# Three convolution steps among the gates of a fused convolution and feed-forward kernel: behind units 1, 5 and 9 in place of 1, 3 and 5

## The chip, the cores and the metric

The kernel runs on one core of one Trainium2 chip. The metric is the device time of one execution in microseconds. A profiled execution gives every instruction of the five engines: TensorE (PE, with its weight loads as PEld), VectorE (DVE), ScalarE (ACT), GpSimd (POOL) and SyncE (SP), which issues transfers here.

## The reference

Two blocks in a row, in float32:

```
# x: (8, 4096, 192), weight: (8, 7)
w = softmax(weight, axis=-1)
out[b, s, d] = sum_k w[head(d), k] * x_padded[b, s + k, d]     # causal, 7 taps, 8 heads of 24 channels

# tokens: 8 * 4096 = 32768, w_in: (192, 2048), w_out: (2048, 192)
h = out.reshape(32768, 192) @ w_in
g = h * clip(h + 3, 0, 6) / 6                                    # hardswish
return g @ w_out
```

## The kernel before, in words

The 32768 tokens are taken in 32 blocks of 1024. A block has two groups of 512 tokens, which lie in the lower and the upper 64 partitions. The first block (number 0) has a path of its own with the preparation of the weights. Blocks 1 to 31 go through the same two stages, which are the 31 iterations of the loop at the end of the kernel.

**The first layer** (`first_layer`) computes h and the gate. It has 16 units, 8 with the tokens as they lie (`y_own`) and 8 with the two groups swapped (`y_other`). Each unit makes 128 features for both groups. A float32 product is made of three parts in a 32-bit format for TensorE: `HIGH`, `LOW` and `MIX`. `begin(n)` takes a pair of PSUM banks, issues the 12 matmuls of HIGH and LOW (L510) and scales the sum on ScalarE (L521). `end(n)` adds the 6 matmuls of MIX, then clamps on ScalarE (`relu`, L302) and multiplies on VectorE (`gate`, L306). The gate reads the pair of banks; when it has ended, the pair is free. There are four pairs. TensorE's order is begin(0), begin(1), and then end(n), begin(n + 2) for each n, but begin(15) comes ahead of end(13). So begin(n + 4) waits for gate n.

**The sums of gates.** Both layers' products are organised in a Strassen-like way with fewer products and more sums. Behind units 1, 3, 5 and 7 GpSimd makes `small_sums` (L573, four instructions each) of the two units just gated. Behind units 9, 11 and 13 it makes a sum `g_sums` (L414), and behind 9 and 11 it also issues a transfer that adds one part of g onto another (L552). VectorE makes that sum behind unit 15.

**The second layer** (`second_layer`) multiplies by `w_out` (L609), sums the parts, transposes and stores. Its order is written out by hand with due times. VectorE has most of its sums there (L573, L414, L458), and also splits the next block's y into its three parts (L877, L479).

**The convolution** of block i + 1 runs on VectorE during block i. Its seven steps go through the whole of `y` (128 partitions x 1536). The first is a scaled copy on ScalarE (L859), and the other six are multiply-adds on VectorE, in place, one tap each (L861):

```
            for k in range(1, KC):
                jobs.append(lambda k=k: nc.vector.scalar_tensor_tensor(
                    out=y[:], in0=x[:, :, k : k + N], scalar=c_sb[:, k : k + 1], in1=y[:],
                    op0=ALU.mult, op1=ALU.add,
                ))
```

Steps 1 and 2 are done at the end of the second layer. Step 3 comes ahead of the first gate, with two last output sums of the block before (`left`). Steps 4, 5 and 6 are `conv[4:]`, handed to `first_layer` as `jobs`, a table from unit to what follows its gate. The order of every engine's queue is the order in which the kernel issues (a manual schedule): each engine takes its instructions one after the other.

Of the kernel before, what the change touches and what calls it, by code (L numbers as in the profile page):

```python
# [25 lines left out]
def kernel(  # L26
# [50 lines left out]
    def load_x(i, dma=nc.sync):  # L77
        x = xs.tile([P, K3, PAD + N], F32, name="x")
        head, lower, upper = x_source(i)
        if head:  # L80
            nc.vector.memset(x[0:D2, :, 0:PAD], 0.0)
        dma.dma_start(out=x[0:D2, :, head:], in_=lower)
        dma.dma_start(out=x[D2:P, :, :], in_=upper)
        return x
# [655 lines left out]
    with tc.manual_schedule():  # L740
# [82 lines left out]
        n = 3  # L823
# [33 lines left out]
        def conv_jobs(i):  # L857
            x = x_tiles.pop(i)
            jobs = [lambda: nc.scalar.mul(y[:], x[:, :, 0:N], c_sb[:, 0:1])]  # L859
# [5 lines that stand above are left out]
            return jobs  # L865
# [35 lines left out]
        conv = conv_jobs(2)  # L901
        conv[0]()
        left = conv[1:3]
        for i in range(1, NB):
            jobs = {2 * n + 1: [job] for n, job in enumerate(conv[4:])}
            jobs[-1] = left + conv[3:4]
            first_layer(i, jobs)
            conv = []

            def begin_conv():  # L910
                x_tiles[i + 2] = load_x(i + 2)
                conv.extend(conv_jobs(i + 2))

            between = []
            if i + 1 < NB:
                between = [(13, split_high), (15, split_rest), (18, swap_parts)]
            if i + 2 < NB:
                between += [(20, begin_conv), (60, lambda: conv[0]()), (72, lambda: conv[1]()), (73, lambda: conv[2]())]
            left = second_layer(i, between)
# [33 lines left out]
```

## Time and profile before

| | us |
|---|---|
| device time, median of 3 runs (2244.72 to 2244.84) | 2244.84 |
| span of the profiled execution | 2244.1 |
| one iteration, from the chain of waits (237.99 to 306.94 is one) | 68.95 |
| of it the second layer on TensorE (216 pieces in the chain) | 35.47 |
| of it the first layer on TensorE, the rest | 33.48 |
| convolution step on VectorE (L861), least, median, longest | 1.774, 1.820, 2.249 |
| gate on VectorE (L306), median | 1.220 |
| clamp on ScalarE (L302), mean in the groups of the page | 1.088 |

How to read it: TensorE's row says where the time is, because the whole span is TensorE's stream, one iteration after the other. The other engines' rows only matter where they make TensorE wait. A line of a timeline has the start, the length, the engine, the line of the kernel, the operation, what it writes and reads, how many instructions are merged into it, and in brackets the idle time ahead of it with the one that ended it. In a table of waits the columns are the total, the number of times and, where there is one, the longest.

### The profile page before, as it was taken

What the parts mean: (1) busy time and instruction counts of PE and PEld (TensorE: products, weight loads), DVE (VectorE), ACT (ScalarE), POOL (GpSimd) and SP (SyncE); (2) the same over time, 40 slices, a digit from 0 to 9 for tenths busy, and PEclk for the clock granted to TensorE, in tenths of its full rate; (3) what the DMA queues carried; (4) which work ended last, traced back from release to release, by engine and by line L of the source; (5) the groups of instructions that cost most, each with busy time, mean ns of one, the idle gap of its engine ahead of it and who ended that gap; (6) DMA issues with size and microseconds to landing.
All of it is one profiled execution on the core that took longest, in us unless ns stands there. A gap on an engine that the chain in (4) does not pass through costs nothing.

```text
span 2244.1 us, 50173 instructions
## 1 busy us (share of the span) xinstructions
PE 2233.8 (100%) x21432; PEld 1525.2 (68%) x21432; DVE 1890.1 (84%) x1636; ACT 1388.8 (62%) x1676; POOL 825.0 (37%) x689
## 2 busy tenths in 40 slices
PE   9999999999999999999999999999999999999998
PEld 5467776676766667766767667676666776676765
DVE  8888888888898888888888888889888888888876
ACT  7457665576655676555766556665567655576653
POOL 2444432344422444323443224442244432344322
PEclk9999999999999999999999999999999999999999
DMA  6344224443234342344423443323434234443332
GB/s 155 71 84 83 48 58 91 86 81 64 54 79 91 78 80 46 68 90 83 84 51 60 85 89 78 70 52 74 90 79 85 46 62 90 84 83 55 58 69 34
DMA packets 254063, 166.57 MB, mean 74 GB/s; under 512 B 208528, under 2 KB 213648, under 8 KB 253840
## 3 DMA queue, kind: packets, MB, share of 16 engines
q1 hardware_dynamic: 235416, 129.53, 28.3%
q0 software_dynamic: 17184, 33.57, 8.6%
q8 instruction: 168, 2.75, 0.5%
q14 instruction: 55, 0.45, 0.1%
q10 hardware_dynamic: 1240, 0.27, 0.1%
HBM read 31.72 MB, written 25.17 MB: 25 GB/s over the span
## 4 chain that ended last, share of the span: by engine, by line
PE 98%; DVE 1%; ACT 0%; issue 0%; DVEq 0%; ACTq 0%
PE psum L609 49%; PE psum L510 44%; PE psum L296 2%; PE psum L341 2%; DVE g L306 1%; DVE y L861 1%; PE psum L755 0%; PE psum L763 0%; ACT g L302 0%; DVE results L458 0%; ACT psum L521 0%; DVE results L464 0%; ACT results L709 0%; DVE zeros L111 0%; DVEq L464 0%
## 5 line engine op out<-in xcount | busy, mean ns | idle before, releaser
L609 PE MATMUL psum<-g,w_out 128*32 128x512 f32 (+1 forms) x6696 | 967.3, 553 | 0.0
L306 DVE SCALAR_TENSOR_TENSOR g<-g,psum 128x1024 f32<-128x1024 f32 (+1 forms) x528 | 611.9, 1183 | 224.4 <-ACT g L302 220.0
L573 POOL TENSOR_TENSOR s<-g 128x256 f32<-128x256 f32 x248 | 318.8, 1285 | 1213.6 <-DVE g L306 1213.6
L302 ACT ACTIVATE g<-psum,half 128x1024 f32<-128x1024 f32 (+1 forms) x528 | 564.7, 1088 | 0.8
L521 ACT ACTIVATE psum<-psum 128x1024 f32<-128x1024 f32 x496 | 500.2, 1009 | 74.9 <-PE psum L510 72.0
L609 PEld LDWEIGHTS psum<-g,w_out 128*32 128x32 f32 x6696 | 370.0, 110 | 247.0 <-issue 127.9
L510 PE MATMUL psum<-y_other,w_in 64*128 64x512 f32 x4464 | 530.6, 390 | 1.3
L510 PE MATMUL psum<-y,w_in 64*128 64x512 f32 x4464 | 521.9, 388 | 0.0
L510 PEld LDWEIGHTS psum<-y,w_in 64*128 64x128 f32 x4464 | 413.7, 184 | 116.3 <-issue 25.1
L510 PEld LDWEIGHTS psum<-y_other,w_in 64*128 64x128 f32 x4464 | 411.3, 184 | 110.3 <-DVE g L306 22.1
L609 PE MATMUL psum<-s,w_out 128*32 128x512 f32 (+1 forms) x3224 | 465.4, 576 | 0.0
L861 DVE SCALAR_TENSOR_TENSOR y<-x,c_sb,y 128x1536 f32<-128x1536 f32 x186 | 360.5, 1938 | 1.3
L609 PE MATMUL psum<-g,w_s 128*32 128x256 f32 x1240 | 282.8, 379 | 0.0
L414 POOL TENSOR_TENSOR s<-g 128x1024 f32<-128x1024 f32 x93 | 224.6, 2415 | 67.2 <-DVE g L306 67.2
L609 PEld LDWEIGHTS psum<-s,w_out 128*32 128x32 f32 x3224 | 152.5, 110 | 81.7 <-issue 50.0
L609 PEld LDWEIGHTS psum<-g,w_s 128*32 128x32 f32 x1240 | 136.4, 110 | 67.8
L414 DVE TENSOR_TENSOR s<-g 128x2048 f32<-128x2048 f32 (+1 forms) x93 | 179.4, 1957 | 1.1
L609 PE MATMUL psum<-s,w_s 128*32 128x256 f32 x744 | 170.7, 379 | 0.0
L573 DVE TENSOR_TENSOR g<-g 128x1024 f32<-128x1024 f32 x124 | 151.7, 1224 | 5.2
L414 DVE TENSOR_TENSOR g<-g 128x2048 f32<-128x2048 f32 x62 | 139.1, 2284 | 0.0
L606 ACT COPY psum<-psum 32x512 f32<-32x512 f32 x93 | 51.3, 551 | 132.7 <-PE psum L609 132.7
L458 DVE TENSOR_TENSOR results<-psum,results 32x256 f32<-32x256 f32 (+1 forms) x125 | 68.0, 544 | 48.4 <-issue 47.0
(82 smaller groups left out, 1266.6 us busy)
## 6 DMA issues: line engine op xcount, KB each, us to landing
y_other<-y SPq DMA_DIRECT2D x186, 384.0 KB, 5.1
g<-g POOLq DMA_DIRECT2D x62, 512.0 KB, 5.0
out_dram<-results SPq DMA_DIRECT2D x378, 64.0 KB, 2.0
x<-in_x_dram SPq DMA_DIRECT2D x53, 388.5 KB, 7.7
stage<-in_moe_w_in_dram SPq DMA_DIRECT2D x16, 192.0 KB, 4.5
stage<-in_moe_w_out_dram SPq DMA_DIRECT2D x8, 384.0 KB, 5.2
x<-in_x_dram SPq DMA_DIRECT2D x7, 384.0 KB, 8.4
x<-in_x_dram POOLq DMA_DIRECT2D x2, 388.5 KB, 5.8
```

The lines of the kernel that those rows point to most:

```text
L296: nc.tensor.matmul(out=psum[:, b], lhsT=w[r], rhs=src, start=start, stop=stop, skip_group_check=onto,)
L302: nc.scalar.activation(r6, h, ACT.Relu, bias=half[:], scale=1.0 / 6.0)
L306: nc.vector.scalar_tensor_tensor(out=g_, in0=g_, scalar=1.0, in1=h, op0=ALU.min, op1=ALU.mult)
L341: lambda p=p: nc.tensor.matmul(out=bank[j * QS : (j + 1) * QS, tokens], lhsT=w_out[:, p, w, cols], rhs=x[:, p, tokens], start=(first and p ...
L414: engine.tensor_tensor(out=o[:, r], in0=a[:, r], in1=b[:, r], op=op)
L458: nc.vector.tensor_tensor(out=out, in0=x, in1=y, op=op)
L510: nc.tensor.matmul(out=psum[:, 2 * slots[n] + k], lhsT=r32(w_in_parts[part][r, c, s]), rhs=r32(y_other[0][r, part, s] if group else y_own[ ...
L521: nc.scalar.mul(both(n), both(n), 4097.0)
L573: engine.tensor_tensor(out=o, in0=p, in1=q, op=op)
L606: streams[3].append((t - 0.5, lambda: fn(*args, **kw)))
L609: nc.tensor.matmul(out=out, lhsT=w, rhs=x, start=start, stop=True, tile_position=(0, j * QS), skip_group_check=True,)
L861: jobs.append(lambda k=k: nc.vector.scalar_tensor_tensor(out=y[:], in0=x[:, :, k : k + N], scalar=c_sb[:, k : k + 1], in1=y[:], op0=ALU.mu ...
```

## The change

In each iteration the steps 4, 5 and 6 of the convolution follow other gates. Before, they came behind the gates of units 1, 3 and 5. Now they come behind those of units 1, 5 and 9. What is computed, and the order of the six steps among themselves, stays. The purpose is to spread VectorE's work in the first layer: two gates stand between two steps before, and four now.

```diff
         for i in range(1, NB):
-            jobs = {2 * n + 1: [job] for n, job in enumerate(conv[4:])}
+            jobs = {4 * n + 1: [job] for n, job in enumerate(conv[4:])}
             jobs[-1] = left + conv[3:4]
             first_layer(i, jobs)
```

The orders of TensorE, ScalarE, GpSimd and SyncE are the same in both kernels. Only VectorE's differs. Its queue in the first layer, one iteration, by lines of the kernel:

```
before:  L306 x2, L861, L306 x2, L861, L306 x2, L861, L306 x10
after:   L306 x2, L861, L306 x4, L861, L306 x4, L861, L306 x6
```

## The prediction

> **What bounds the kernel now.** I read four views in this order: the page's busy shares, the chain of waits, the table of waits, and the timeline of one of the 31 repeated iterations, engine by engine. The page first:
>
> ```profile
> PE 2233.8 (100%) x21432; PEld 1525.2 (68%) x21432; DVE 1890.1 (84%) x1636; ACT 1388.8 (62%) x1676; POOL 825.0 (37%) x689
> PEclk9999999999999999999999999999999999999999
> PE 98%; DVE 1%; ACT 0%; issue 0%; DVEq 0%; ACTq 0%
> ```
>
> TensorE carries 98% of the chain at full clock. Only holes in its stream can be won, and a busy share of 100% with modelled ends hides them. The table of waits, kept to weight loads, lists them:
>
> ```profile
> PEld psum L510 <- issue: 25.1, 30, 0.8
> PEld psum L510 <- DVE g L306: 22.7, 61, 0.5
> PEld psum L510 <- ACT psum L521: 5.2, 31, 0.2
> ```
>
> 61 times a first-layer weight load waits for a gate (L306): the gate frees the PSUM pair that the unit four later writes. That wait is what the change can reach. One iteration's weight loads show its size:
>
> ```profile
> 1148.98 0.64 PEld L510 LDWEIGHTS psum<-y,w_in 64*128 64x128 f32 x6
> 1149.90 1.23 PEld L510 LDWEIGHTS psum<-y_other,w_in 64*128 64x128 f32 x12 [0.28 <-DVE g L306]
> 1151.17 0.65 PEld L510 LDWEIGHTS psum<-y,w_in 64*128 64x128 f32 x6
> 1151.86 2.00 PEld L510 LDWEIGHTS psum<-y_other,w_in 64*128 64x128 f32 x18
> 1154.33 0.75 PEld L510 LDWEIGHTS psum<-y_other,w_in 64*128 64x128 f32 x8 [0.47 <-DVE g L306]
> ```
>
> Loads come in pairs, one for each half of the rows. Nine pairs take 2.04 us (this is the spacing of units everywhere between the stalls), so 0.227 us a pair. The third pair of the first line starts at 1148.98 + 2 x 0.227 = 1149.43; the next is due at 1149.66 and comes at 1149.90: 0.24 us lost, in front of unit 8. The ninth pair from 1151.86 starts at 1153.68; the next is due at 1153.90 and comes at 1154.33: 0.42 us lost, in front of unit 10. The idle times in brackets are some 0.04 us above the loss each, which is the ordinary hole between two pairs. So the 61 waits cost about 22.7 - 61 x 0.043 = 20.1 us.
>
> Why VectorE is late, from its own timeline and GpSimd's:
>
> ```profile
> 1142.47 1.81 DVE L861 SCALAR_TENSOR_TENSOR y<-x,c_sb,y 128x1536 f32<-128x1536 f32 x1
> 1144.20 2.37 DVE L306 SCALAR_TENSOR_TENSOR g<-g,psum 128x1024 f32<-128x1024 f32 x2
> 1146.49 2.23 DVE L861 SCALAR_TENSOR_TENSOR y<-x,c_sb,y 128x1536 f32<-128x1536 f32 x1
> 1148.64 2.34 DVE L306 SCALAR_TENSOR_TENSOR g<-g,psum 128x1024 f32<-128x1024 f32 x2
> 1150.90 2.24 DVE L861 SCALAR_TENSOR_TENSOR y<-x,c_sb,y 128x1536 f32<-128x1536 f32 x1
> 1153.06 2.34 DVE L306 SCALAR_TENSOR_TENSOR g<-g,psum 128x1024 f32<-128x1024 f32 x2
> 1158.08 1.22 DVE L306 SCALAR_TENSOR_TENSOR g<-g,psum 128x1024 f32<-128x1024 f32 x1 [1.15 <-ACT g L302]
> 1160.15 1.22 DVE L306 SCALAR_TENSOR_TENSOR g<-g,psum 128x1024 f32<-128x1024 f32 x1 [0.85 <-ACT g L302]
> ```
>
> ```profile
> 1142.63 2.25 POOL L573 TENSOR_TENSOR s<-g 128x256 f32<-128x256 f32 x1 [40.23 <-DVE g L306]
> 1144.96 0.75 POOL L573 TENSOR_TENSOR s<-s,g 128x256 f32<-128x256 f32 x1
> 1147.05 2.27 POOL L573 TENSOR_TENSOR s<-g 128x256 f32<-128x256 f32 x1
> 1158.12 0.75 POOL L573 TENSOR_TENSOR s<-g,s 128x256 f32<-128x256 f32 x1
> 1159.38 2.41 POOL L414 TENSOR_TENSOR s<-g 128x1024 f32<-128x1024 f32 x1 [0.51 <-DVE g L306]
> ```
>
> Two gates (2.34 us) and a step (2.24 us) need about 4.4 us from step to step (1146.49 to 1150.90), while TensorE makes two units in 4.08. Three steps in a row build a backlog. In the second half of the stage VectorE waits 0.8 to 1.15 us before each gate: the room is there.
>
> **What the Trainium skill says.** "SBUF — State Buffer", section "Who interferes with whom": a VectorE instruction with two SBUF inputs contends with a GpSimd instruction that reads SBUF, and whichever issues first keeps the shared port for its whole length. The trace agrees. The step at 1142.47, ahead of GpSimd's, takes 1.81 us and stretches that one from 0.75 to 2.25; the steps at 1146.49 and 1150.90 meet a GpSimd instruction under way and take 2.23. Gates, with one input in PSUM, stay at 1.22. "TensorE: Matmul & The Clock Gate", section "Back-to-back issue gap", gives 518 cycles for an isolated 512-column matmul at 2.4 GHz, 0.216 us; the trace's pair takes 0.227, and I use the trace.
>
> **The change part by part.** Nothing is added or removed, and only VectorE's queue is reordered: the step behind unit 3 goes behind 5, and the one behind 5 goes behind 9. No other engine's order changes.
>
> First the allowance. The ScalarE clamp (L302) of unit 4 ends at 1147.36, and clamps follow each other by 2.04 (starts 1148.29, 1150.33). Call the end R(n): R(4) = 1147.36, R(5) = 1149.40, R(6) = 1151.44, R(9) = 1157.56, R(10) = 1159.60 without stalls. Unit 8 is due at 1149.66, some 0.05 after gate 4 must end: a gate has until R + 2.25. Alone it ends at R + 0.04 + 1.22 = R + 1.26. So gate n has 0.99 us to spare, plus what gate n-1 leaves.
>
> Step behind 1: as now. Gate 2 starts at 1144.20, ends at 1145.41 = R(2) + 2.13, within 2.25, and no stall stands there today.
>
> Step behind 3, taken away: gate 4 starts at R(4) + 0.04 and ends at 1148.62 instead of 1149.85. The 0.24 us before unit 8 goes.
>
> Step behind 5: gate 5 ends at 1150.66 and the step starts 0.08 before that, at 1150.58. GpSimd's small sums of units 2 and 3 start at about 1147.05, no longer stretched, and 4 x 0.70 us later, at 1149.9, they are done. So the step finds the port free and takes 1.81, to 1152.39. Gate 6 starts 0.08 earlier and ends at 1153.53 = R(6) + 2.09. Unit 10 is due at 1153.74, allowing for no earlier stall, and gate 6 needs to end by 1153.69: 0.16 to spare. The 0.42 us goes.
>
> Step behind 9: gate 9 ends at 1158.82, the step starts at 1158.74. The small sums of units 6 and 7 start behind those of 4 and 5 at 1155.2 and end at 1158.0, 0.7 before it. The GpSimd sum (L414) that waits for gate 9 starts 0.08 after that gate's end, so 0.16 after the step: the order of 1142.47 and 1142.63 again. The step runs 1.81 us, gate 10 ends at R(10) + 2.09, and unit 14 isn't held.
>
> What is queued behind this step: gates 10 to 15 on VectorE. Gate 11 is due at R(11) + 1.26 and follows gate 10 without loss, so unit 15, which is taken ahead of the end of unit 13, has 0.3 us more than its gate needs. On GpSimd the sum of 2.41 us is held until 1160.55 and ends near 1162.9 instead of 1161.80. Then an accumulating transfer is issued (0.30 + 1.21), the next sum runs to about 1166.9, and its transfer is issued by 1168.4 where 1167.39 stands now; with 5.0 us to landing it is there by about 1172.5. VectorE reads these sums at 1178.07 now, 1177.4 then: 5 us to spare. The last GpSimd sum then starts at about 1168.6 and ends near 1171.0; VectorE's own sum, ready at 1170.5, may wait 0.5 us for the port. VectorE waits 0.1 and 0.2 us in the second layer at 1179 and 1180.8, which takes up most of that, and its product sums (two of 2.3 us from 1184.13) still end about a microsecond ahead of their use. I cost all this at nothing.
>
> Sum: in iterations 2 to 30 both stalls go, 29 x 0.66 = 19.2 us. Iteration 1 has three (0.39, 0.17 and 0.34 us by the same reading); the first two come from five VectorE instructions and a step in front of gate 0 and stay, the third goes. Iteration 31 has no steps and no stall today. 19.2 + 0.34 = 19.5 us; 2244.84 - 19.5 = 2225.3.
>
> **The rivals.** (a) Half a gain: the allowance of 0.16 us isn't enough, or a GpSimd instruction is under way when a moved step starts, as for 2.23-us steps today. Each of the two moved steps then costs up to 0.24 us: 30 x 0.48 = 14.4 of the 19.5 come back, 2239.7. For it: the allowance is thin. Against: gate 2 makes do with 0.12 in every iteration.
> (b) Nothing: the gates come earlier but TensorE meets another wait one step on, for instance ScalarE, whose two instructions fill 2.04 us of every 2.04. Against: the only such wait shown is 5.2 us in all, with the last unit. It would give 2244.8.
> (c) Slower: GpSimd's sum wins the port before the step behind 9. The step waits until 1158.90 + 2.41 = 1161.31 and ends at 1163.1, gate 10 at 1164.2 against an allowance of 1161.85: 2.35 us x 30 = 70 less the 19.5, 2295. Against: VectorE starts its next instruction before the last one's recorded end, GpSimd 0.08 after it.
>
> **How the numbers follow.** Full gain 0.80, (a) 0.08, (b) 0.04, (c) or a late sum in the second layer 0.08. The forecast is 2225.3. The low end is the removal of every gate stall, 2224.7, with a margin for the reading, 2223.0. The high end allows each of the three steps 0.1 us over the allowance, 30 x 0.3 = 9 us: 2234.5. (b) and (c) and the full size of (a) lie outside, 0.20. Faster: 0.80 + 0.08 = 0.88; same 0.04; slower 0.08.
>
> **What would show it.** Right: waits of L510 for gates fall from 61 to about 2, and from 22.7 to under 1 us; all three steps last about 1.8 us; the first layer falls from 33.44 to about 32.8 us and the second stays at 35.5; the first GpSimd sum (L414) stretches to about 4 us. Wrong: a step of 2.2 us or more behind 5 or 9, a new wait of L510 or L609 for VectorE or GpSimd, or a longer second layer.

## The result and the profile after

The changed kernel takes 2230.24 us (median of 6, 2230.07 to 2230.50) against 2244.81 us (median of 6, 2244.52 to 2245.09): 14.6 us less, ratio 0.9935, 95% interval 0.9922 to 0.9948. The forecast was 2225.3 us in a range of 2223.0 to 2234.5.

The page of the changed kernel, the lines that answer to those of before:

```profile
PE 2219.4 (100%) x21432; PEld 1528.0 (69%) x21432; DVE 1872.5 (84%) x1636; ACT 1390.0 (62%) x1676; POOL 827.7 (37%) x689
PEclk9999999999999999999999999999999999999999
PE 100%; DVE 0%; issue 0%; ACT 0%; DVEq 0%
```

VectorE has left the chain of waits. The table of waits of the weight loads (total, times, longest):

```profile
PEld psum L510 <- issue: 26.0, 31, 0.8
PEld psum L510 <- ACT psum L521: 10.3, 62, 0.2
PEld psum L510 <- DVE g L306: 1.1, 3, 0.5
```

Of 61 waits for a gate 3 are left, all in iteration 1. The other waits were there before. ScalarE's row had 31 times and has 62, because a second hole of each iteration, ahead of the MIX part of unit 0, was 0.146 us and is 0.166, and only now the table lists it.

Where the time came from, in the chain of waits. First before, then after, two neighbouring stages of each (start, length, what):

```profile
1134.14 20.15 PE psum L510 x174
1154.28 0.04 issue
1154.33 13.27 PE psum L510 x114
1167.60 35.47 PE psum L609 x216
```

```profile
1058.24 32.92 PE psum L510 x288
1091.17 35.47 PE psum L609 x216
```

The second layer is 35.47 us in both. The first layer is 33.46 us before and 32.92 after: 0.54 us in each of iterations 2 to 30, 15.7 in all, which is the difference of the two profiled spans (2244.1 and 2228.4). The profiled execution of before was 1.3 us above the median of its kernel (2246.07 against 2244.81) and that of the changed kernel 0.3 above (2230.50 against 2230.24), so the medians differ by a little less, 14.6.

VectorE in the first layer of a later iteration of the changed kernel, and GpSimd beside it, from the timeline:

```profile
1134.95 1.81 DVE L861 SCALAR_TENSOR_TENSOR y<-x,c_sb,y 128x1536 f32<-128x1536 f32 x1
1143.06 1.81 DVE L861 SCALAR_TENSOR_TENSOR y<-x,c_sb,y 128x1536 f32<-128x1536 f32 x1
1144.79 2.43 DVE L306 SCALAR_TENSOR_TENSOR g<-g,psum 128x1024 f32<-128x1024 f32 x2
1151.22 1.81 DVE L861 SCALAR_TENSOR_TENSOR y<-x,c_sb,y 128x1536 f32<-128x1536 f32 x1
1152.95 2.44 DVE L306 SCALAR_TENSOR_TENSOR g<-g,psum 128x1024 f32<-128x1024 f32 x2
```

```profile
1141.76 0.74 POOL L573 TENSOR_TENSOR s<-g,s 128x256 f32<-128x256 f32 x1
1143.22 2.25 POOL L573 TENSOR_TENSOR s<-g 128x256 f32<-128x256 f32 x1 [0.73 <-DVE g L306]
1149.86 0.74 POOL L573 TENSOR_TENSOR s<-g,s 128x256 f32<-128x256 f32 x1
1151.39 3.92 POOL L414 TENSOR_TENSOR s<-g 128x1024 f32<-128x1024 f32 x1 [0.79 <-DVE g L306]
```

All three steps last 1.81 us. GpSimd has been idle for 0.73 and 0.79 us when its next sum is released, so the two moved steps find it at rest and start 0.16 us ahead of it. Then GpSimd waits: one sum is 2.25 us long instead of 0.74, and the sum for units 8 and 9 is 3.92 instead of 2.41. The transfer behind that sum is issued later for it, but no load or matmul waits for GpSimd here.

### The profile page after: what moved, and what is told of

Same layout as the page of the kernel before. It is cut to its first block, busy times and chain, and to the rows that moved or that the text cites. A ratio compares the mean times of both kernels' runs of the same rounds, so it can differ in the third digit from the quotient of the medians.

```text
span 2228.4 us, 50173 instructions
## 1 busy us (share of the span) xinstructions
PE 2219.4 (100%) x21432; PEld 1528.0 (69%) x21432; DVE 1872.5 (84%) x1636; ACT 1390.0 (62%) x1676; POOL 827.7 (37%) x689
## 4 chain that ended last, share of the span: by engine, by line
PE 100%; DVE 0%; issue 0%; ACT 0%; DVEq 0%
PE psum L609 49%; PE psum L510 46%; PE psum L296 2%; PE psum L341 2%; PE psum L755 0%; PE psum L763 0%; DVE results L458 0%; DVE results L464 0%; ACT results L709 0%; DVE zeros L111 0%; DVEq L464 0%; DVE x L96 0%; DVE half L233 0%; DVE bias_e L150 0%; DVE bias_e L149 0%
## 5 line engine op out<-in xcount | busy, mean ns | idle before, releaser
L306 DVE SCALAR_TENSOR_TENSOR g<-g,psum 128x1024 f32<-128x1024 f32 (+1 forms) x528 | 618.1, 1186 | 228.2 <-ACT g L302 223.9
L573 POOL TENSOR_TENSOR s<-g 128x256 f32<-128x256 f32 x248 | 271.6, 1095 | 1232.3 <-DVE g L306 1232.3
L510 PE MATMUL psum<-y,w_in 64*128 64x512 f32 x4464 | 521.7, 388 | 0.0
L510 PE MATMUL psum<-y_other,w_in 64*128 64x512 f32 x4464 | 517.0, 386 | 0.0
L510 PEld LDWEIGHTS psum<-y,w_in 64*128 64x128 f32 x4464 | 413.3, 184 | 116.1 <-issue 26.0
L510 PEld LDWEIGHTS psum<-y_other,w_in 64*128 64x128 f32 x4464 | 415.7, 184 | 91.0 <-ACT psum L521 5.1
L861 DVE SCALAR_TENSOR_TENSOR y<-x,c_sb,y 128x1536 f32<-128x1536 f32 x186 | 336.1, 1807 | 1.3
L414 POOL TENSOR_TENSOR s<-g 128x1024 f32<-128x1024 f32 x93 | 282.7, 3040 | 30.2 <-DVE g L306 30.2
```

The lines of the kernel that those rows point to most:

```text
L306: nc.vector.scalar_tensor_tensor(out=g_, in0=g_, scalar=1.0, in1=h, op0=ALU.min, op1=ALU.mult)
L414: engine.tensor_tensor(out=o[:, r], in0=a[:, r], in1=b[:, r], op=op)
L510: nc.tensor.matmul(out=psum[:, 2 * slots[n] + k], lhsT=r32(w_in_parts[part][r, c, s]), rhs=r32(y_other[0][r, part, s] if group else y_own[ ...
L573: engine.tensor_tensor(out=o, in0=p, in1=q, op=op)
L861: jobs.append(lambda k=k: nc.vector.scalar_tensor_tensor(out=y[:], in0=x[:, :, k : k + N], scalar=c_sb[:, k : k + 1], in1=y[:], op0=ALU.mu ...
```

## The experiments

**What makes a gate late: the number of gates between two steps, or GpSimd?** Both fit the result. The spacing theory says that three steps with two gates between them are too much by themselves. The port theory says that they are too much only because a step that meets a GpSimd instruction which reads SBUF is held up. With the order of before, two gates and a step needed 4.4 us against 4.08, but two of the steps took 2.23 us instead of 1.81. The cleanest test keeps the order of before and takes away what GpSimd reads.

```diff
-                small_sums(s1[-1], A11, (1, 2, 3, 4), nc.gpsimd, every[n - 1 : n + 1])
+                nc.gpsimd.memset(s1[-1][:, n - 1 : n + 1], 0.0)
```

> The order of before (1, 3, 5), with the GpSimd small sums of the first layer left out: a GpSimd memset of their destination stands in their place, which reads nothing. Port theory: all three steps take about 1.8 us, two gates and a step then need 2.34 + 1.81 - 0.08 = 4.07 us against 4.08, gates 4 and 6 come in time, the waits of L510 for gates fall from 61 to about 2, and the time is that of the changed kernel, 2229 to 2231. Spacing theory: steps that follow each other with two gates between still pile up, most of the 61 waits stay, 2238 to 2245.

> The control: the changed order (1, 5, 9) with the same small sums left out. Both theories: nothing is left to win by them, so the time is that of the changed kernel within 1 us, 2229 to 2231; were it much lower, the left-out work would have cost something of its own and the run with the order of before couldn't be read.

The first took 2229.97 us (ratio 0.9934, 0.9919 to 0.9949), the control 2229.94. VectorE with the order of before, in a first layer of the first run:

```profile
1202.96 1.81 DVE L861 SCALAR_TENSOR_TENSOR y<-x,c_sb,y 128x1536 f32<-128x1536 f32 x1
1204.69 2.38 DVE L306 SCALAR_TENSOR_TENSOR g<-g,psum 128x1024 f32<-128x1024 f32 x2
1207.00 1.81 DVE L861 SCALAR_TENSOR_TENSOR y<-x,c_sb,y 128x1536 f32<-128x1536 f32 x1
1208.73 2.43 DVE L306 SCALAR_TENSOR_TENSOR g<-g,psum 128x1024 f32<-128x1024 f32 x2
1211.08 1.81 DVE L861 SCALAR_TENSOR_TENSOR y<-x,c_sb,y 128x1536 f32<-128x1536 f32 x1
```

Steps behind units 1, 3 and 5, and none is stretched: they start 4.04 and 4.08 us apart, at the pace of two units. Two waits of L510 for gates are left, both in iteration 1:

```profile
PEld psum L510 <- DVE g L306: 0.6, 2, 0.4
```

So the distance of two gates was enough by itself; the loss before came from the steps that met GpSimd's reads. The control shows that the left-out sums cost nothing of their own. The memsets don't wait for gates, so they run early and are over before the second and the third step; GpSimd is idle beside those two. But they lay beside the first step:

```profile
1201.38 3.64 POOL L547 MEMSET s<- 128x1024 f32 x4 [38.45 <-DMA out_dram<-results]
```

They write from 1201.38 to 1205.02 and the step at 1202.96 keeps its 1.81 us, as do all 28 steps of this run that start beside such a memset. So GpSimd doesn't hold this step up when it only writes. The Trainium skill ("SBUF — State Buffer", section "Who interferes with whom") says that a VectorE instruction with two SBUF inputs contends with a GpSimd instruction that reads SBUF and not with one that only writes it. The trace of before agrees on the first (2.23 us), this one on the second (1.81).

**Each step by itself.** In one run only the last of the three steps is moved (1, 3, 9; its edit stands here). In the other the last step is put where GpSimd works (1, 5, 7):

```diff
-            jobs = {4 * n + 1: [job] for n, job in enumerate(conv[4:])}
+            jobs = {n: [job] for n, job in zip((1, 3, 9), conv[4:])}
```

> Steps behind units 1, 3 and 9: only the third step is moved. Port theory (a step that meets a GpSimd sum under way takes 2.2 us and makes the next gate late): the step behind 3 stays at 2.23 us, the weight load before unit 8 stays 0.24 us late in each iteration, that before unit 10 is on time. If a late weight load costs the matmuls its whole lateness, the kernel is 30 x 0.24 = 7.2 us above the changed kernel, 2237.5; if the loads run ahead of the matmuls by some 0.1 us and only the rest counts, 30 x 0.16 = 4.8, 2235.0.

It took 2234.30 us (0.9953, 0.9937 to 0.9970). The step behind 3 takes 2.21 us, those behind 1 and 9 take 1.81. From iteration 2 on one late load an iteration is left, before unit 8, 0.23 us late, and the first layer is 0.148 us longer than the changed kernel's (means of iterations 2 to 30). Iteration 1 is 0.18 us shorter. 29 x 0.148 - 0.18 = 4.1, and 4.1 were measured: so it is the smaller of the two costs expected.

> Steps behind units 1, 5 and 7: the third step starts while GpSimd is still at the small sums of units 4 and 5. Port theory: it takes 2.3 to 2.4 us, gate 8 ends about 2.63 us after its clamp against an allowance of 2.25, the load before unit 12 is 0.4 us late in each iteration, and the time is 2238 to 2242. Spacing theory (only a backlog of three steps with two gates between each delays a gate): two steps make no stall, 2230.

It took 2232.97 us (0.9948, 0.9933 to 0.9963). That lies above the 2230 of the spacing theory and below the 2238 to 2242 of the port theory, whose size was missed: the effect is there, but smaller. VectorE, then GpSimd:

```profile
1216.56 2.16 DVE L861 SCALAR_TENSOR_TENSOR y<-x,c_sb,y 128x1536 f32<-128x1536 f32 x1
```

```profile
1212.64 2.25 POOL L573 TENSOR_TENSOR s<-g 128x256 f32<-128x256 f32 x1 [0.73 <-DVE g L306]
1216.36 0.75 POOL L573 TENSOR_TENSOR s<-g,s 128x256 f32<-128x256 f32 x1
1217.06 2.27 POOL L573 TENSOR_TENSOR s<-g 128x256 f32<-128x256 f32 x1
```

The step starts 0.20 us after GpSimd's last sum of units 4 and 5, which has 0.55 us to go, and takes 0.35 us longer than alone. So gate 8 is late by less than I had worked out (2.3 to 2.4 us for the step), and the load before unit 12 is 0.18 us late instead of 0.4. The row of 2.25 us shows how one step sets up the next: the step behind 5 holds GpSimd's sums back by 1.5 us, so that they are still under way two units later.

**A place that looks free and isn't.**

```diff
+            jobs = {n: [job] for n, job in zip((1, 5, 10), conv[4:])}
```

> Steps behind units 1, 5 and 10. Unit 15 is taken ahead of the end of unit 13, so gate 11 has 0.68 us less than the others, 1.57 us after its clamp. A step of 1.8 us in front of it ends it at 2.09, and GpSimd's sum for units 8 and 9 (2.4 us from gate 9 on) is still under way when the step starts, so it takes 2.2 to 2.35 and gate 11 ends at 2.5 to 2.6. Allowance and port together: the load before unit 15 is 0.9 to 1.0 us late, 30 x 0.85 = 25 us above the changed kernel, 2253 to 2258. If only the port mattered (allowance 2.25 as for the others): 0.3 us late, 2237. If only the number of gates between two steps mattered: 2230.

It took 2254.72 us beside 2245.67 of the kernel before on the same chip, so it is slower than before (1.0042, 1.0027 to 1.0057). VectorE, GpSimd and the weight loads there:

```profile
1234.64 2.15 DVE L861 SCALAR_TENSOR_TENSOR y<-x,c_sb,y 128x1536 f32<-128x1536 f32 x1
1236.70 2.34 DVE L306 SCALAR_TENSOR_TENSOR g<-g,psum 128x1024 f32<-128x1024 f32 x2
```

```profile
1232.76 2.40 POOL L414 TENSOR_TENSOR s<-g 128x1024 f32<-128x1024 f32 x1 [0.79 <-DVE g L306]
```

```profile
1234.86 2.23 PEld L510 LDWEIGHTS psum<-y_other,w_in 64*128 64x128 f32 x20
1237.96 3.29 PEld L510 LDWEIGHTS psum<-y_other,w_in 64*128 64x128 f32 x30 [0.88 <-DVE g L306]
```

One unit later than behind 9, the step finds the 2.40-us sum under way until 1235.16 and takes 2.15 us. Gate 11 behind it ends at 1237.9, and unit 15, taken ahead of the end of unit 13, has waited 0.88 us for it. Both parts of the expectation hold, the port and the shorter allowance.

**What a meeting costs.** The stretched steps fit one sum. In the trace of before 62 steps last longer than 1.9 us, and each lasts 1.81 us plus what the GpSimd instruction under way still has left when the step starts, less 0.19 to 0.20 us. The steps of before at 1146.49 and 1150.90 met these two:

```profile
1146.36 0.75 POOL L573 TENSOR_TENSOR s<-g,s 128x256 f32<-128x256 f32 x1
1150.79 0.73 POOL L573 TENSOR_TENSOR s<-g,s 128x256 f32<-128x256 f32 x1
```

Both have 0.62 us left, and 1.81 + 0.62 - 0.20 = 2.23. The 99 stretched steps of the three runs with other places fit as well. Where only 0.16 and 0.18 us were left (in iteration 1 of the runs 1, 5, 7 and with 4 memsets), the step kept its 1.81 us. This fits a port that stays with the instruction under way to its end, but for 0.2 us by the records; where the 0.2 us come from isn't shown.

**What a late load costs.** In the changed kernel, memsets of one column were put between the step behind 9 and gate 10: 4, 8 (as here) and 16 of them:

```diff
+            if 9 in jobs:
+                jobs[9] += 8 * [lambda: nc.vector.memset(bias_e[:, 0:1], 0.0)]
             jobs[-1] = left + conv[3:4]
```

> The changed kernel with 4 one-column memsets of a constant that is no longer read, on VectorE between the step behind unit 9 and gate 10, in each iteration. Such a memset takes 0.059 us in the trace, so gate 10 ends some 0.24 us later, 2.32 us after its clamp against an allowance of 2.25, and the load before unit 14 is about 0.07 us late. If the loads run ahead of the matmuls by some 0.1 us and only the rest counts (from the two runs with other places of the steps: 0.225 late cost 0.140, 0.177 late cost 0.080), this costs nothing: 2230.2. If the whole lateness counts, 30 x 0.07 = 2.1 us more: 2232.3.

> The same with 8 memsets: gate 10 ends 0.47 us later, the load before unit 14 is about 0.30 us late. With 0.09 us free: 30 x 0.21 = 6.3 us more, 2236.5. With the whole lateness: 30 x 0.30 = 9 us more, 2239.2.

> The same with 16 memsets: gate 10 ends 0.94 us later, the load before unit 14 is about 0.77 us late. With a fixed 0.09 us free: 30 x 0.68 = 20.4 us more, 2250.6. With the whole lateness: 2253.3. If a late load also gave back a share of its lateness that grows with it, less than 2248.

They took 2235.49, 2251.46 and 2281.34 us, beside 2245.67 of the kernel before on the same chip (ratios 0.9956, 1.0025 and 1.0158; intervals 0.9939 to 0.9973, 1.0015 to 1.0035, 1.0143 to 1.0173). All lie far above what was expected, because a memset costs twice what its record says. Two of eight, from the timeline:

```profile
1164.01 0.18 DVE L907 MEMSET bias_e<- 128x1 f32 x2
```

Two of them fill 0.18 us, so each starts 0.12 us after the one ahead, although a record is 0.059 us long. The loads confirm it: 4 memsets more make them 0.50 us later, 8 more another 1.01. The sizes were wrong, but the runs still give what they were made for. The table has how late the load is (the hole between two pairs of loads, less 0.227) and how much longer the loads of the first layer take from first to last than in the changed kernel (32.38 us). All are means of iterations 2 to 30, with the least and the most of single iterations in brackets:

| run | load late, us | first layer longer, us | difference |
|---|---|---|---|
| steps 1, 5, 7 | 0.176 | 0.099 (0.060 to 0.133) | 0.077 |
| gate 10 later, 4 | 0.218 | 0.167 (0.117 to 0.213) | 0.051 |
| steps 1, 3, 9 | 0.230 | 0.148 (0.139 to 0.180) | 0.082 |
| before (two waits) | 0.242 + 0.426 | 0.532 (0.530 to 0.564) | 0.136 |
| gate 10 later, 8 | 0.718 | 0.672 (0.638 to 0.718) | 0.046 |
| steps 1, 5, 10 | 0.842 | 0.784 (0.757 to 0.830) | 0.058 |
| gate 10 later, 16 | 1.727 | 1.683 (1.638 to 1.711) | 0.044 |

A late load costs its lateness less 0.04 to 0.08 us, and that discount doesn't grow with the lateness. Neither theory had it exactly: whole lateness is wrong, and a constant 0.09 is too much. Up to 0.02 us of a difference doesn't come from the late load: the hole ahead of the MIX part of unit 0 is that much shorter in some of the runs (0.333 us from pair to pair in before, 0.353 in the changed kernel).

Where the discount comes from stands in the traces. This is the wait before unit 8 in before (matmuls and loads):

```profile
1149.66 0.39 PE L510 MATMUL psum<-y,w_in 64*128 64x512 f32 x2
1149.90 0.53 PEld L510 LDWEIGHTS psum<-y_other,w_in 64*128 64x128 f32 x6 [0.28 <-DVE g L306]
1149.90 0.73 PE L510 MATMUL psum<-y_other,w_in 64*128 64x512 f32 x4
```

The load at 1149.90 is 0.24 us late. The pairs of loads behind it follow faster at first: three pairs take 0.53 us where 2 x 0.227 + 0.184 = 0.64 is usual. The second pair of matmuls starts at 1149.90 + 0.73 - 0.39 = 1150.24 instead of 1150.11, so of the 0.24 us 0.13 are lost there. In six waits looked at, two in before and one each in the runs 1, 3, 9 and 1, 5, 7 and with 8 and 16 memsets, the load pair behind the late one makes up 0.12 us, whether the load was 0.17 or 1.72 us late. Over the next ten pairs or so, some of which start 0.229 us apart instead of 0.227, 0.03 to 0.05 us of that is lost again. Why was not found.

## Why the prediction was right, and where it was off

Right in direction and within its range; the gain was 14.6 us where 19.5 was forecast.

- **The bound and the waits.** TensorE's stream is all there is, and the 61 waits for gates were what could be won. They went to 3 (forecast: about 2), and nothing else in the chain took their place.
- **The step behind 1** stayed as it was, the steps behind 5 and 9 take 1.81 us as worked out, and the margins held: gate 6 ends 2.07 us after its clamp and gate 10 2.08, where 2.09 was forecast and 2.25 allowed. No load waits for them from iteration 2 on. The mechanism was the one forecast, a moved step that finds the port free, so the direction was not luck.
- **GpSimd behind unit 9.** Forecast: held for 1.6 us, some 4 us long, and harmless. Measured: 3.92 us long, no load waits for it, second layer 35.47 us as before. The half microsecond allowed for VectorE's own sum didn't come.
- **The step that failed in size** is "0.24 us lost" and "0.42 us lost", hence 29 x 0.66, written as 19.2 (it is 19.1). The lateness of a load was taken for the loss of the stream. The loads were late by that much, but the layer lost only 0.53 us for the two of them, because the load pair behind a late one makes up 0.12. So the term is 29 x 0.53 = 15.4, 3.8 less. The 20.1 us for all 61 waits has the same error.
- **Iteration 1.** The third of its waits was forecast to go, 0.34 us. It moved instead: the first layer of iteration 1 is as long after as before (33.09 us from first to last load). The small sums start later there against the gates (the first at 113.19, behind gate 3; in before it is the same, at 113.07; the cause stays open). So the step behind 9 meets them under way and takes 2.40 us, and unit 14 waits for gate 10:

```profile
124.99 2.40 DVE L861 SCALAR_TENSOR_TENSOR y<-x,c_sb,y 128x1536 f32<-128x1536 f32 x1
```

```profile
125.04 0.74 POOL L573 TENSOR_TENSOR s<-g 128x256 f32<-128x256 f32 x1
```

  That is rival (a), in one iteration of 30. The two runs without the small sums lack this wait, and they are 0.3 us faster than the changed kernel.
- 19.5 - 3.8 - 0.3 = 15.4, against 15.7 between the profiled spans. The remaining microsecond to the medians comes from the profiled executions, of which that of before was longer than usual. Where in the run it was longer is not shown.
- **Why the gates were late** was put half wrong: "Three steps in a row build a backlog" was true only with the stretched steps. The run with the order of before and no reads by GpSimd shows that the same three steps in the same places cost no wait from iteration 2 on.
- Rivals (b) and (c) didn't occur. For (c), the lead of 0.16 us was enough in iterations 2 to 30. In iteration 1 it is another matter: the step at 124.99 starts 0.05 us ahead of GpSimd's next sum (125.04), and its 2.40 us fit if that sum still went first (its end lies 0.79 us behind the step's start, and 1.81 + 0.79 - 0.20 = 2.40). So a lead of 0.05 us by the records was not enough there.

## What to carry to other kernels

In a kernel like this one, place a VectorE instruction with two SBUF inputs where GpSimd doesn't read SBUF. A good place is behind the very instruction that releases GpSimd's next one: here VectorE went first by 0.16 us, and GpSimd took the wait, for which it had the slack. Count VectorE's own work with the durations of undisturbed instructions, and look for two different durations of the same instruction before blaming the order. Read the loss of a wait from the distance of whole units or stages, not from the hole in the loads.

## What the runs showed that was not expected

In a row of memsets to the same column, a one-column memset on VectorE occupies 0.12 us from start to start with a record of 0.059 us, so 16 of them made a load 1.73 us late, where 0.77 was expected from their records. A step that met a GpSimd sum paid just what that sum had left, less 0.20 us. And from iteration 2 on GpSimd's reads were the entire loss: 2229.97 us with the order of before and no reads by the small sums, against 2229.94 with the changed order and none.
